# Moving the output weights' block sums beside the second sequence, and its output product to Strassen's form, in a fused attention and SwiGLU kernel

## The chip, the cores and the metric

The kernel runs on one core of one Trainium2 chip. The metric is the time of one execution on the device in microseconds, lower is better. Executions of one kernel agree within about 0.3%. The profile is of one execution: TensorE is PE (PEld its weight loads), VectorE is DVE, ScalarE is ACT, GpSimd is POOL, SyncE, which issues the transfers, is SP.

## The reference, cut to what matters

```python
batch, n_heads, seq, head_dim = (8, 12, 448, 64)
q_n, k_n = rmsnorm(q, g_q), rmsnorm(k, g_k)
scores = scale * q_n @ k_n.T                    # softmax, then @ v
x = attn_out ...reshape(8 * 448, 768)
xn = x / rms(x) * rms_g
g, val = xn @ w_gate, xn @ w_val                # 768 -> 1536
out = (silu(g) * val) @ w_out                   # 1536 -> 768
```

All is in float32. The weights arrive as float64 and are converted on the chip.

## The kernel before

The eight sequences go through a pipeline: while TensorE does the attention of a later sequence, pieces of the feed-forward part of an earlier one are put between ("items"). The first sequence's products are plain, because its weights are still being converted. From the second on, gate and value products are in Strassen's (Winograd's) form, which needs seven block products instead of eight and pays for it with sums and differences of blocks; there are six groups of seven, called quads here. Each quad needs four derived weight blocks (T1 to T4), made on VectorE beside the second sequence, stored to DRAM, and loaded again for every later sequence.

The output product was plain for the first two sequences and in Strassen's form from the third (`FIRST_O = 2`). Its derived blocks, 24 in all, were made in place beside the third sequence:

```python
    FIRST_O = 2
    uses = []                                   # the order in which blocks are loaded
    for b in range(1, B):
        for fp in range(NFP):                   # NFP = 6
            if b == 2:
                uses += [("wd", b, name, fp) for name in BLOCKS]
            uses += [("w", b, fp, name, w) for name in (...) for w in range(2)]
        if b < FIRST_O:
            uses += [("wo", b, *block_of(n, fc)) ...]          # plain: 24 blocks
        else:
            uses += [("wo", b, name, c) for name, _ in out_order(b) for c in range(NFP)]
...
    def derive_o(wait=6):
        ...
        a, b = data(("wd", 2, plus, c)), data(("wd", 2, minus, c))
        nc.vector.tensor_tensor(data(key), a, b, ALU.subtract)
        after(1, store)
```

Strassen's form also needs sums of the hidden blocks, made three items after each quad ends:

```python
        def sums():
            for pair in range(1 + b % 2) if b >= FIRST_O else ():
                ...
                nc.vector.tensor_tensor(of("S1"), of("A21"), of("A22"), ALU.add)
                nc.vector.tensor_tensor(of("S2"), of("S1"), of("A11"), ALU.subtract)
                nc.vector.tensor_tensor(of("S3"), of("A11"), of("A21"), ALU.subtract)
                nc.vector.tensor_tensor(of("S4"), of("A12"), of("S2"), ALU.subtract)
```

In a quad, three PSUM banks go round. VectorE adds each product to running sums (`u` and `cc`, `c` in the profile), which frees its bank; the last product is added by TensorE onto a bank that VectorE must have read before. And the loop that issues an item:

```python
            while asked["derived"] < sums_made:
                derive(0)
                ask()
            pe(fn)
            convert()
            derive()
            derive()
            derive_o()
```

## Time and profile before

| | |
|---|---|
| time, median of the first three runs | 1637.91 us (1637.1 to 1639.52) |
| span of the profile | 1636.9 us |
| TensorE busy | 1615.2 us |
| VectorE, ScalarE, GpSimd busy | 862.6, 499.8, 631.3 us |
| moved by DMA | 273.28 MB |

"Busy" of TensorE is the time covered by its instructions, which overlap. How fast it works is read from how far apart instructions start. The lines are in the prediction.

### The profile page before, as it was taken

What the parts mean: (1) busy time and instruction counts of PE and PEld (TensorE: products, weight loads), DVE (VectorE), ACT (ScalarE), POOL (GpSimd) and SP (SyncE); (2) the same over time, 40 slices, a digit from 0 to 9 for tenths busy, and PEclk for the clock granted to TensorE, in tenths of its full rate; (3) what the DMA queues carried; (4) which work ended last, traced back from release to release, by engine and by line L of the source; (5) the groups of instructions that cost most, each with busy time, mean ns of one, the idle gap of its engine ahead of it and who ended that gap; (6) DMA issues with size and microseconds to landing.
All of it is one profiled execution on the core that took longest, in us unless ns stands there. A gap on an engine that the chain in (4) does not pass through costs nothing.

```text
span 1636.9 us, 21470 instructions
## 1 busy us (share of the span) xinstructions
PE 1615.2 (99%) x7376; PEld 1142.1 (70%) x7376; DVE 862.6 (53%) x1371; ACT 499.8 (31%) x975; POOL 631.3 (39%) x569
## 2 busy tenths in 40 slices
PE   6999999999999999999999999999999999999998
PEld 3444445678855888568875688758876587969984
DVE  6988998366542476426562354624555234433431
ACT  6756563233222332223223222322232123100110
POOL 6777777334423343334433333344343322100000
PEclk9999999999999999999999999999999999999999
DMA  7757674454613866665544655466454464557652
GB/s 195 227 158 204 183 228 128 141 185 142 211 51 117 254 203 222 204 196 162 154 139 120 196 154 159 119 204 192 146 148 124 151 192 114 146 179 241 174 150 65
DMA packets 246443, 273.28 MB, mean 167 GB/s; under 512 B 66356, under 2 KB 243252, under 8 KB 246324
## 3 DMA queue, kind: packets, MB, share of 16 engines
q1 hardware_dynamic: 246004, 271.80, 55.8%
q8 instruction: 61, 1.00, 0.3%
q14 instruction: 58, 0.48, 0.1%
q10 hardware_dynamic: 320, 0.00, 0.0%
HBM read 232.40 MB, written 39.32 MB: 166 GB/s over the span
## 4 chain that ended last, share of the span: by engine, by line
PE 92%; DVE 4%; DMA 2%; ACT 1%; SPq 0%; POOL 0%; issue 0%; DVEq 0%; ACTq 0%; POOLq 0%
PE ff L793 41%; PE ff L987 18%; PE sc L476 9%; PE av L501 8%; PE ff L888 7%; PE den L512 3%; PE ff L1018 2%; PE tr L461 2%; DVE top L646 1%; DVE top L644 1%; DVE top L645 1%; DVE rd L520 1%; DMA qk<-in_k_dram 1%; ACT e L480 1%; DMA raw<-in_moe_w_out_dram 0%; DMA raw<-in_moe_w_gate_dram 0%
## 5 line engine op out<-in xcount | busy, mean ns | idle before, releaser
L793 PE MATMUL ff<-x,w 128*128 128x224 f32 x2016 | 405.7, 353 | 0.0
L793 PEld LDWEIGHTS ff<-x,w 128*128 128x128 f32 x2016 | 378.5, 190 | 12.0 <-issue 6.6
L793 PE MATMUL ff<-xs,w 128*128 128x224 f32 x1512 | 308.0, 353 | 0.0
L793 PEld LDWEIGHTS ff<-xs,w 128*128 128x128 f32 x1512 | 283.4, 190 | 5.3 <-issue 5.3
L480 ACT ACTIVATE e<-sc,rs 112x448 f32<-112x448 f32 x384 | 212.0, 635 | 194.4 <-PE sc L476 189.3
L486 POOL TENSOR_TENSOR es<-e 112x448 f32<-112x448 f32 x82 | 95.1, 1181 | 455.9 <-ACT e L480 455.9
L490 POOL TENSOR_TENSOR es<-es,e 112x448 f32<-112x448 f32 x164 | 187.2, 1152 | 85.3 <-ACT e L480 78.8
L520 DVE RECIPROCAL rd<-rd 128x448 f32<-128x448 f32 x41 | 121.1, 2952 | 143.2 <-ACT rd L519 143.2
L987 PE MATMUL ff<-w,h 128*128 128x384 f32 x576 | 191.1, 487 | 0.0
L476 PE MATMUL sc<-qkT 64*112 64x448 f32 x768 | 179.0, 571 | 5.1 <-ACT qkT L464 5.1
L987 PEld LDWEIGHTS ff<-w,h 128*128 128x128 f32 x576 | 108.1, 190 | 75.5 <-issue 4.0
L501 PE MATMUL av<-e,vt 112*64 112x448 f32 x768 | 154.9, 545 | 0.0
L444 POOL TENSOR_TENSOR rs<-ms,mhalf 112x16 f32<-112x16 f32 (+1 forms) x50 | 143.4, 2867 | 4.2
L476 PEld LDWEIGHTS sc<-qkT 64*112 64x112 f32 x768 | 69.4, 174 | 98.0 <-issue 70.6
L501 PEld LDWEIGHTS av<-e,vt 112*64 112x64 f32 x768 | 50.8, 136 | 95.3 <-issue 75.2
L1018 PE MATMUL ff<-x,w 128*128 128x448 f32 x288 | 112.0, 542 | 0.0
L888 PE MATMUL ff<-w,h 128*128 128x384 f32 x336 | 111.0, 488 | 0.0
L987 PE MATMUL ff<-w,so 128*128 128x384 f32 x324 | 108.6, 488 | 2.0 <-DVE y L948 2.0
L805 DVE TENSOR_TENSOR cc<-ff,u 128x448 f32<-128x448 f32 x84 | 52.4, 624 | 90.4 <-PE ff L793 90.0
L888 PEld LDWEIGHTS ff<-w,h 128*128 128x128 f32 x336 | 62.8, 190 | 43.7 <-issue 2.7
L987 PEld LDWEIGHTS ff<-w,so 128*128 128x128 f32 x324 | 60.5, 190 | 44.7 <-DVE y L948 3.9
L1018 PEld LDWEIGHTS ff<-x,w 128*128 128x128 f32 x288 | 53.3, 190 | 50.8 <-issue 48.8
(86 smaller groups left out, 1470.5 us busy)
## 6 DMA issues: line engine op xcount, KB each, us to landing
w<-kept SPq DMA_DIRECT2D x552, 192.0 KB, 3.3
w<-kept_o SPq DMA_DIRECT2D x318, 192.0 KB, 3.0
kept<-w SPq DMA_DIRECT2D x96, 192.0 KB, 3.8
qk<-in_q_dram SPq DMA_DIRECT2D x48, 224.0 KB, 3.4
qk<-in_k_dram SPq DMA_DIRECT2D x96, 112.0 KB, 3.9
vt<-in_v_dram SPq DMA_DIRECT2D x48, 224.0 KB, 2.8
raw<-in_moe_w_gate_dram SPq DMA_DIRECT2D x24, 384.0 KB, 4.4
raw<-in_moe_w_val_dram SPq DMA_DIRECT2D x24, 384.0 KB, 4.7
```

The lines of the kernel that those rows point to most:

```text
L444: nc.gpsimd.tensor_tensor(st["rs", g][:, cols], ms, mhalf[0:P, cols], ALU.pow)
L476: nc.tensor.matmul(ps[0:P, 0:S], lhsT=qkT[r, 1, c * P:(c + 1) * P], rhs=qkT[r, 0, :], start=True, stop=True)
L480: nc.scalar.activation(e, ps[0:P, 0:S], ACT.Exp, scale=rs[:, n:n + 1])
L486: nc.gpsimd.tensor_tensor(es, st["e", g, 0, j], st["e", g, 1, j], ALU.add)
L490: nc.gpsimd.tensor_tensor(es, es, st["e", g, c, j], ALU.add)
L501: nc.tensor.matmul(av[j * D:(j + 1) * D, 0:S], lhsT=vt[:, j, c, :], rhs=st["e", g, c, j], start=(c == 0), stop=(c == NT - 1))
L520: nc.vector.reciprocal(rd, rd)
L793: nc.tensor.matmul(bank[:, w * HT:(w + 1) * HT], lhsT=wt[:, c * 128:(c + 1) * 128], rhs=x[:, c, :], start=onto is None and w == c == 0, st ...
L805: nc.vector.tensor_tensor(add[name], ps[:, 0:S], add[other], ALU.add)
L888: nc.tensor.matmul(ps, lhsT=st["h", b, fc][:, i * 128:(i + 1) * 128], rhs=data(("wo", b, *block_of(n, fc))), start=(fc == 0), stop=(fc == ...
L987: nc.tensor.matmul(ps, lhsT=a, rhs=data(("wo", b, name, c)), start=first and c == 0, stop=c == NFP - 1, skip_group_check=True)
L1018: nc.tensor.matmul(bank[w][:, 0:S], lhsT=data(key)[:, c * 128:(c + 1) * 128], rhs=st["x", 0, half][:, c, :], start=half == c == 0, stop=ha ...
```

## The change

The intent is to have the output weights' derived blocks one sequence earlier, so that the second sequence's output product takes 84 instead of 96 matmuls. The extra blocks need room, so the four buffers of the weight conversion become block places when the conversion has ended.

```diff
@@ convert
+        if turn_of["n"] == TURNS:
+            free_w.extend(cv_pool.tile([128, BW], F32, name="top") for _ in range(4))
@@
-    FIRST_O = 2
+    FIRST_O = 1
@@ order of loads
-            if b == 2:
+            uses += [("w", b, fp, name, w) for name in (...) for w in range(2)]
+            if b == 1:
                 uses += [("wd", b, name, fp) for name in BLOCKS]
-            uses += [("w", b, fp, name, w) for name in (...) for w in range(2)]
@@ ask
-            if key[1] == 1 and key[0] == "w":
-                keep_free = 7 + 8 * key[2] - asked["derived"]
+            if key[1] == 1 and key[0] in ("w", "wd"):
+                fp = key[2] if key[0] == "w" else key[3]
+                keep_free = max(7 + 8 * fp - asked["derived"], 1)
@@ derive_o: every ("wd", 2, ...) becomes ("wd", 1, ...)
@@ fill
             while asked["derived"] < sums_made:
+                n = asked["derived"]
                 derive(0)
                 ask()
+                if n == asked["derived"]:
+                    pe(idle)
```

More of the change, by code (lines that the diff above doesn't have):

```diff
@@ L706, in safe_scores @@
         for fp in range(NFP):
-            if b == 2:
+            uses += [("w", b, fp, name, w) for name in (("B12", "B11", "B22", "B21") if b == 1 else ORDER) for w in range(2)]
+            if b == 1:
                 uses += [("wd", b, name, fp) for name in BLOCKS]
-            uses += [("w", b, fp, name, w) for name in (("B12", "B11", "B22", "B21") if b == 1 else ORDER) for w in range(2)]
         if b < FIRST_O:
@@ L763, in derive_o @@
         for name in BLOCKS:
-            if asked.get(("wd", 2, name, c), now["t"]) > now["t"] - wait:
+            if asked.get(("wd", 1, name, c), now["t"]) > now["t"] - wait:
                 return
         sums_o.pop(0)
-        a, b = data(("wd", 2, plus, c)), data(("wd", 2, minus, c))
-        key = ("wd", 2, to, c)
-        st[key] = st[("wd", 2, place, c)]
+        a, b = data(("wd", 1, plus, c)), data(("wd", 1, minus, c))
+        key = ("wd", 1, to, c)
+        st[key] = st[("wd", 1, place, c)]
         nc.vector.tensor_tensor(data(key), a, b, ALU.subtract)
@@ L778, in derive_o @@
             for name in ("T1", "T2", "T3", "T4"):
-                after(6, lambda name=name: used(("wd", 2, name, c)))
+                after(6, lambda name=name: used(("wd", 1, name, c)))
     def used(key):
```

## The prediction

> **What bounds the kernel now.** I read the page's first two parts, then the table of what each engine waited for, then the chain that ended last, and then one stage at a time.
>
> ```profile
> span 1636.9 us, 21470 instructions
> ...
> PE 1615.2 (99%) x7376; PEld 1142.1 (70%) x7376; DVE 862.6 (53%) x1371; ACT 499.8 (31%) x975; POOL 631.3 (39%) x569
> ...
> PE tr L461 <- POOL ms L441: 5.5, 1, 5.5
> PE sc L476 <- ACT qkT L464: 5.1, 2, 4.4
> PE ff L987 <- DVE y L948: 2.0, 3, 0.7
> PE tr L461 <- POOL qn L448: 1.9, 1, 1.9
> PE den L512 <- ACT e L480: 1.0, 3, 0.5
> ```
>
> TensorE is idle for 1636.9 - 1615.2 = 21.7 us in all. The waits listed make 15.5 us; the two large ones and the 1.9 us are the very first transposes and scores. The rest, some 6 us, follows the last matmul. Over the 1600 us between, TensorE waits about 3 us. So the time is the sum of what TensorE does, and a change pays by the matmuls it takes out, less any wait that it brings in. No line of this table has TensorE waiting for a weight block's transfer.
>
> What a matmul costs is read from the groups and from the chain, whose columns are start, length, piece:
>
> ```profile
> L793 PE MATMUL ff<-x,w 128*128 128x224 f32 x2016 | 405.7, 353 | 0.0
> L793 PE MATMUL ff<-xs,w 128*128 128x224 f32 x1512 | 308.0, 353 | 0.0
> L987 PE MATMUL ff<-w,h 128*128 128x384 f32 x576 | 191.1, 487 | 0.0
> ...
> L888 PE MATMUL ff<-w,h 128*128 128x384 f32 x336 | 111.0, 488 | 0.0
> ...
> 451.12 7.76 PE ff L888 x24
> ...
> 659.86 7.76 PE ff L987 x24
> ```
>
> The mean of one instruction, 488 ns, is not its cost: neighbours overlap. The cost is the pace, 7.76/24 = 0.323 us for one of 384 columns, the same in the plain product (L888) and in Strassen's form (L987). The trace has each matmul of the program as two instructions: the plain products of sequences 0 and 1 are (3 + 4) x 2 x 12 = 168 matmuls, and the row says 336.
>
> The third reading is by stage: the second sequence's gate and value products (321 to 451 us), its output (to 537), the third sequence's gate and value products (537 to 657), its output, and the fourth's (722 to 842). The columns are stretch, length, busy us of each engine, clock, DMA share and GB/s.
>
> ```profile
> 321.00:451.00 130.00, 130.00 (x697) 110.06 (x696) 79.60 (x125) 38.71 (x77) 54.34 (x51) 1.00 0.58 179
> 451.00:537.00 86.00, 86.00 (x319) 45.76 (x318) 28.89 (x33) 20.30 (x38) 26.15 (x22) 1.00 0.33 95
> 537.00:657.00 120.00, 120.00 (x643) 104.97 (x644) 72.68 (x122) 34.32 (x68) 46.27 (x38) 1.00 0.73 227
> ...
> 722.00:842.00 120.00, 120.00 (x640) 100.05 (x638) 66.15 (x117) 37.85 (x74) 47.57 (x50) 1.00 0.55 158
> ```
>
> TensorE is full in each. VectorE is at 61% where the change will put more on it, and there it is already close behind TensorE at times:
>
> ```profile
> 403.62 0.62 DVE L527 TENSOR_TENSOR x<-av,rd 128x448 f32<-128x448 f32 x1
> 404.17 0.61 DVE L805 TENSOR_TENSOR cc<-ff,u 128x448 f32<-128x448 f32 x1
> 404.70 2.19 DVE L750 TENSOR_TENSOR w<-w,w 128x384 f32<-128x384 f32 x2
> 406.81 0.61 DVE L805 TENSOR_TENSOR c<-ff,u 128x448 f32<-128x448 f32 x1
> ```
>
> There is no idle time before any of these four: for some microseconds VectorE runs behind.
>
> **What the Trainium skill says.** "Perfetto Trace Analysis", section "Tensor Engine Instruction (MATMUL, LD_WEIGHTS)", says that VectorE's queue is strictly first in, first out, and that TensorE's ends are modelled. The first means that an added subtraction delays whatever stands behind it, also a sum that TensorE needs; the four lines above, back to back, agree. "SBUF — State Buffer", section "Who interferes with whom", says that a VectorE instruction with two SBUF inputs contends with a GpSimd instruction that reads SBUF, and one with a single SBUF input does not. All the VectorE work added in the loaded stage has two SBUF inputs. The trace agrees: a pair of block subtractions (L750) takes 2.19 us at 404.70 and 1.02 us at 421.37, and in the fourth sequence a 128x128 sum takes 1.22 us at 766.47 but 0.28 us at 751.41. "DMA: Bandwidth & Descriptors", section "Anatomy of one DMA — SWDGE (gpsimd) path", fits a transfer as 2.0 us plus its bytes at 436 GB/s, which for a 192 KB block would be an estimated 2.45 us; the fit is for the other queue, and the trace's own medians, 3.0 to 3.8 us from issue to landing, are used here.
>
> **The change, part by part.**
> Removed: the plain output product of the second sequence, 4 row tiles x 2 halves x 12 = 96 matmuls. Put in: 2 pairs x 7 products x 6 = 84. The built programs agree: 618 matmuls of 384 columns become 606, and every other matmul count is equal. 12 matmuls x 2 x 0.323 = 7.76 us less TensorE work, all of it on the path; the stage of 86 us should come down to about 78.
> Moved: the 24 subtractions of output weight blocks, their 24 loads and 24 stores go from the third sequence to the second. In the order of the changed program 4 come before the quads of the second sequence and 20 beside them. At the third sequence's rate (20 took 12.8 us of VectorE) that is 12.8 us.
> Added on VectorE: 48 sums of hidden blocks (128x128) for the two pairs, some 40 of them beside those quads. In the fourth sequence 40 such took 3.6 + 4.8 + 4.8 + 3.8 = 17.0 us. VectorE in the second sequence's stage thus goes from 79.6 to about 79.6 + 12.8 + 17.0 = 109 of 130 us, 84%.
> Added transfers: 42 blocks instead of 24 are read for that output, 18 x 0.197 MB = 3.5 MB more over the run. In the stage it is 40 more transfers of 0.197 MB: 7.9 MB on top of 179 GB/s x 130 us = 23.3 MB, about 240 GB/s.
> Four conversion buffers become block places, 27 to 31. By the program's order loads then stand some 40 us of TensorE work ahead of use in the third sequence's quads, before about 23. TensorE waited for none of them, so this buys no time by itself; it makes room for the output blocks among the gate and value blocks. The extra idle steps in the scheduling loop issue no TensorE instruction.
>
> Where can the fuller VectorE hold TensorE? At the product that is added onto a bank after VectorE has read it (B22 onto T1's bank): one product, 6 x 0.379 = 2.3 us, lies between the end of T1 and that need, and the addition takes 0.6 us, so a lag of 1.7 us is free. In the order of the changed program the tightest place is the fifth quad. There VectorE has, from u2 up to that addition: u2 0.53, eight sums 3.4, an output block 0.64, u3 0.53, two halves of the hidden block 0.7, two derived blocks 1.3, a transpose's copy 0.53, the addition 0.53, together 8.2 us. TensorE gets from u2's place to the need in 8.0 us, and about 1.3 us of earlier work is still queued then. So a wait of about 1.5 us is due there; by the same count about half of that in the third quad, and around zero in the others. A GpSimd collision can double any of these instructions. I put the new waits at 2 us, estimated from these rows, with 0.5 to 5 as reasonable.
>
> Sum: 1637.9 - 7.8 + 2.0 = 1632.1 us.
>
> **Rivals.**
> VectorE becomes the bound of the second sequence. For: 84% of a strict queue, with two thirds of the derived blocks in bursts, and every GpSimd collision lengthens it. Against: in the stretch from 82 to 123 us VectorE is busy for 36.5 of 41 us and TensorE does not idle. If all the margin went, 5 to 8 us of waits would cancel the gain: 1635 to 1638.
> The transfers become the bound. For: about 240 GB/s in a stage where VectorE itself waits for blocks, so a late block stops its whole queue. Against: 227 GB/s over the third sequence's 120 us stood beside a full TensorE, and in the changed order the shortest distance from a load to its subtraction is 7 to 8 us there, while landing took 3.7 to 5.3 us. The exceptions, 2 to 3 us for the first subtractions, come some 25 us before TensorE needs them; VectorE waited 4.8 us at that place before as well, harmlessly. If it happened: 1633 to 1637.
> The gain is all kept, 1630.1: if the burst of sums falls into free time, as it does in the fourth sequence, where L793 has no idle at all.
>
> **Range and chances.** Runs of the kernel before spread from 1637.1 to 1639.5. The lower end is the full gain with a favourable run, 1629; the upper end, 1635.5, has the gain eaten by five microseconds of waits. 2% is 33 us, over four times what was taken out, and nothing in the profile can lose as much: 1% faster, 97% within, 2% slower.
>
> **What would show it.** Right: 1,068 Strassen output instructions and 144 plain ones; the second sequence's output stage about 78 us; VectorE near 109 us between 321 and 451; new TensorE waits of 0.5 to 5 us in all, put down to the VectorE addition (cc) and lying between 340 and 435 us; everything after shifted earlier by 5 to 8 us with the stage lengths unchanged. Wrong: TensorE waiting for weight blocks, a second sequence over 135 us, or a pace of the added products that isn't 0.323 us.

## The result, and the profile after

| | before | changed |
|---|---|---|
| median, six runs each on the same chip | 1638.61 us | 1631.05 us |
| lowest to highest | 1637.07 to 1639.56 | 1630.26 to 1632.68 |
| span of the profile | 1636.9 | 1629.0 |
| TensorE busy | 1615.2 | 1607.8 |
| VectorE busy | 862.6 | 871.8 |
| moved by DMA | 273.28 MB | 276.83 MB |

The ratio is 0.9957, 95% interval 0.9944 to 0.997. A ratio is the mean time of one kernel's runs over that of the other's in the same rounds, so it is not quite the ratio of the medians. 0.43% is faster beyond the noise, and "the same" at 2%.

The span and busy times of the changed kernel's page, and, from its table of waits, everything that TensorE waited for (us in total, times, longest):

```profile
span 1629.0 us, 21534 instructions
...
PE 1607.8 (99%) x7352; PEld 1136.8 (70%) x7352; DVE 871.8 (54%) x1425; ACT 499.9 (31%) x975; POOL 632.7 (39%) x569
```

```profile
PE tr L461 <- DMA qk<-in_k_dram: 4.9, 1, 4.9
PE sc L476 <- ACT qkT L464: 3.9, 2, 3.2
PE tr L461 <- POOL qn L448: 2.6, 1, 2.6
PE ff L991 <- DVE y L952: 2.0, 3, 0.7
PE ff L797 <- DVE u L809: 0.8, 1, 0.8
PE ff L797 <- DVE cc L809: 0.4, 1, 0.4
PE den L512 <- ACT e L480: 0.4, 1, 0.4
```

TensorE has 24 instructions fewer. Apart from the first transposes and scores, where the waits change from run to run, there are two new waits against before, both of a quad's product (L797) for a VectorE addition, 0.8 and 0.4 us. No line names a transfer of a weight block. The groups of the output products, plain (L892) and Strassen (L991), count the replacement:

```profile
L991 PE MATMUL ff<-w,h 128*128 128x384 f32 x594 | 202.8, 487 | 0.0
...
L991 PE MATMUL ff<-w,so 128*128 128x384 f32 x338 | 117.3, 488 | 1.4 <-DVE y L952 1.4
...
L892 PE MATMUL ff<-w,h 128*128 128x384 f32 x144 | 47.7, 488 | 0.0
...
L991 PE MATMUL ff<-top,h 128*128 128x384 f32 x78 | 31.9, 490 | 0.0
...
L991 PE MATMUL ff<-top,so 128*128 128x384 f32 x58 | 23.6, 488 | 0.7 <-DVE y L952 0.7
```

594 + 338 + 78 + 58 = 1068 Strassen instructions and 144 plain ones. The name "top" is that of the four new places.

The times of stages are best read from the starts of instructions, because ends are modelled. I use three marks in the timeline of TensorE: the first quad matmul of the second sequence, its first output matmul, and the first output matmul of the third sequence. Stage A is the second sequence's quads; stage B its output product and the third sequence's quads together. B is taken as one because the attention pieces slid across the border between them: the output part alone went from 85.9 to 70.8 us, the quads after it from 122.8 to 130.2.

| | first mark | stage A | stage B |
|---|---|---|---|
| before | 320.72 | 130.24 us | 208.74 us |
| changed | 318.74 | 132.02 us | 201.01 us |

The lines of the three marks, first before and then in the changed kernel:

```profile
320.72 2.45 PE L793 MATMUL ff<-x,w 128*128 128x224 f32 x12
...
450.96 7.92 PE L888 MATMUL ff<-w,h 128*128 128x384 f32 x24
...
659.70 7.92 PE L987 MATMUL ff<-w,h 128*128 128x384 f32 x24
```

```profile
318.74 1.31 PE L797 MATMUL ff<-x,w 128*128 128x224 f32 x6
...
450.76 0.82 PE L991 MATMUL ff<-w,h 128*128 128x384 f32 x2
...
651.77 7.92 PE L991 MATMUL ff<-w,h 128*128 128x384 f32 x24
```

Stage B is 7.73 us shorter, which is the saved matmuls; stage A is 1.78 us longer. Together that is 5.95 us. The other 2 us between the two profiles lie ahead of the first mark, where TensorE has the same work in both: over the profiles, that mark falls anywhere between 317.5 and 321.7 us. So the change is worth about 6 us by the stages. The medians of this pair show 7.6, most likely because they carry the chance of the start as well; the interval of the ratio (4.9 to 9.2 us) holds both.

Where stage A loses its time is in the third quad. First VectorE's timeline in the changed kernel (start, length, instruction, and in brackets the idle time before it), then two lines of GpSimd's, then TensorE's:

```profile
365.31 2.95 DVE L520 RECIPROCAL rd<-rd 128x448 f32<-128x448 f32 x1 [0.40 <-ACT rd L519]
368.36 0.62 DVE L527 TENSOR_TENSOR x<-av,rd 128x448 f32<-128x448 f32 x1
368.90 1.05 DVE L872 TENSOR_TENSOR so<-h,h 128x128 f32<-128x128 f32 x1
370.06 1.49 DVE L873 TENSOR_TENSOR so<-so,h 128x128 f32<-128x128 f32 x1
371.46 1.22 DVE L874 TENSOR_TENSOR h<-h 128x128 f32<-128x128 f32 x1
372.61 0.28 DVE L875 TENSOR_TENSOR so<-h,so 128x128 f32<-128x128 f32 x1
...
373.74 0.55 DVE L754 TENSOR_TENSOR w<-top,w 128x384 f32<-128x384 f32 x1
...
375.14 0.62 DVE L809 TENSOR_TENSOR u<-ff,p 128x448 f32<-128x448 f32 x1
...
378.49 0.61 DVE L809 TENSOR_TENSOR u<-ff,u 128x448 f32<-128x448 f32 x1
...
381.39 0.61 DVE L809 TENSOR_TENSOR cc<-ff,u 128x448 f32<-128x448 f32 x1
```

```profile
366.36 4.64 POOL L490 TENSOR_TENSOR es<-es,e 112x448 f32<-112x448 f32 x4 [1.94 <-ACT e L480]
...
371.32 1.22 POOL L533 TENSOR_TENSOR ss<-ss,rd 128x448 f32<-128x448 f32 x1
```

```profile
379.15 2.54 PE L797 MATMUL ff<-x,w 128*128 128x224 f32 x12 [0.81 <-DVE u L809]
382.06 2.54 PE L797 MATMUL ff<-xs,w 128*128 128x224 f32 x12 [0.37 <-DVE cc L809]
384.43 0.55 PE L461 MATMUL tr<-ident,qk 112*128 112x112 f32 x4
```

VectorE has no idle time from the reciprocal at 365.31 to the addition that ends at 382.0. The first sums of hidden blocks take 1.05, 1.49 and 1.22 us instead of 0.28: GpSimd's four additions of the softmax sums run from 366.36 to 371.0 and another from 371.32 to 372.5. Behind the eight sums and up to the second `u` stand nine subtractions, three of output weight blocks (L774) and six for the quads (L754). Each addition that TensorE needs comes out late. The first wait is for the bank that the second `u` frees; the second is for the `cc` that must be read before the last product.

The idle times shown, 0.81 and 0.37, make 1.18 us; the stage lost 1.78. The dozen behind the second wait is drawn as 2.54 us, but the next instruction starts 2.37 us after it did; a dozen with no break before it is drawn as 2.43 us (at 387.11) and followed after 2.27. So a drawn end lies some 0.17 us late, each wait is shown that much too short, and the dozen behind a break takes 0.10 us longer. A wait thus costs some 0.27 us more than is shown, which makes 1.7 of the 1.78 us.

### The profile page after: what moved, and what is told of

The parts are those of the page before. It is cut to its first block, busy times and chain, and to the rows that moved or that the text cites. A ratio compares the mean times of both kernels' runs of the same rounds, so it can differ in the third digit from the quotient of the medians.

```text
span 1629.0 us, 21534 instructions
## 1 busy us (share of the span) xinstructions
PE 1607.8 (99%) x7352; PEld 1136.8 (70%) x7352; DVE 871.8 (54%) x1425; ACT 499.9 (31%) x975; POOL 632.7 (39%) x569
## 2 busy tenths in 40 slices
DMA packets 249036, 276.83 MB, mean 170 GB/s; under 512 B 66644, under 2 KB 245844, under 8 KB 248916
## 4 chain that ended last, share of the span: by engine, by line
PE 91%; DVE 5%; DMA 2%; ACT 1%; SPq 0%; issue 0%; POOL 0%; DVEq 0%; ACTq 0%; POOLq 0%
PE ff L797 40%; PE ff L991 21%; PE sc L476 9%; PE av L501 9%; PE den L512 3%; PE ff L892 3%; PE ff L1022 2%; PE tr L461 2%; DVE top L646 1%; DVE top L644 1%; DVE rd L520 1%; DVE top L645 1%; ACT e L480 1%; DMA qk<-in_k_dram 1%; DMA raw<-in_moe_w_out_dram 0%; DMA raw<-in_moe_w_gate_dram 0%
## 5 line engine op out<-in xcount | busy, mean ns | idle before, releaser
L797 PE MATMUL ff<-x,w 128*128 128x224 f32 x1728 | 352.3, 354 | 0.8 <-DVE u L809 0.8
L797 PEld LDWEIGHTS ff<-x,w 128*128 128x128 f32 x1728 | 324.1, 190 | 12.1 <-issue 8.6
L797 PE MATMUL ff<-xs,w 128*128 128x224 f32 x1326 | 272.5, 353 | 0.4 <-DVE cc L809 0.4
L797 PEld LDWEIGHTS ff<-xs,w 128*128 128x128 f32 x1326 | 248.7, 190 | 5.4 <-issue 4.7
L991 PE MATMUL ff<-w,h 128*128 128x384 f32 x594 | 202.8, 487 | 0.0
L520 DVE RECIPROCAL rd<-rd 128x448 f32<-128x448 f32 x41 | 121.0, 2952 | 137.6 <-ACT rd L519 137.6
L991 PEld LDWEIGHTS ff<-w,h 128*128 128x128 f32 x594 | 111.5, 190 | 76.6 <-issue 2.7
L991 PE MATMUL ff<-w,so 128*128 128x384 f32 x338 | 117.3, 488 | 1.4 <-DVE y L952 1.4
L991 PEld LDWEIGHTS ff<-w,so 128*128 128x128 f32 x338 | 63.2, 190 | 45.9 <-DVE y L952 2.6
L427 DVE TENSOR_REDUCE ms<-sq 112x8 f32<-112x512 f32 x96 | 61.2, 677 | 52.6 <-ACT sq L424 52.6
L1022 PEld LDWEIGHTS ff<-x,w 128*128 128x128 f32 x288 | 53.3, 190 | 50.9 <-issue 49.0
L682 POOL TENSOR_TENSOR w<-top,raw 128x384 int32<-128x384 int32 x72 | 78.5, 1105 | 25.1 <-DVE top L646 7.3
```

Source lines behind the costliest of these rows:

```text
L427: nc.vector.tensor_reduce(out=ms[:, i * n:(i + 1) * n], in_=sq.rearrange("p (n d) -> p n d", d=D), axis=AX_X, op=ALU.add)
L520: nc.vector.reciprocal(rd, rd)
L682: nc.gpsimd.tensor_tensor(data(key).bitcast(I32), top, lo, ALU.add)
L797: nc.tensor.matmul(bank[:, w * HT:(w + 1) * HT], lhsT=wt[:, c * 128:(c + 1) * 128], rhs=x[:, c, :], start=onto is None and w == c == 0, st ...
L991: nc.tensor.matmul(ps, lhsT=a, rhs=data(("wo", b, name, c)), start=first and c == 0, stop=c == NFP - 1, skip_group_check=True)
L1022: nc.tensor.matmul(bank[w][:, 0:S], lhsT=data(key)[:, c * 128:(c + 1) * 128], rhs=st["x", 0, half][:, c, :], start=half == c == 0, stop=ha ...
```

## The experiments

Theory A is the prediction's: the gain is TensorE's 24 fewer instructions, and the cost is VectorE's fuller queue beside the second sequence. Rivals: blocks arriving earlier give part of the gain (B); the moved subtractions are what costs (C); the new places are not needed (D); the waits are a chance (E); work taken from VectorE comes back through GpSimd (F). Ten runs were made, each kernel in five rounds (e3_no_places has a sixth run) beside the kernel before. "Waits" are the listed ones of the quads' products for VectorE, "VectorE in A" its busy time between the marks of stage A; all in us. Both stages come from the profile of one execution each.

| run | stage A | stage B | VectorE in A | waits | median | ratio to before |
|---|---|---|---|---|---|---|
| before | 130.24 | 208.74 | 79.6 | 0 | | |
| changed | 132.02 | 201.01 | 100.7 | 1.2 | 1631.05 | 0.9957 |
| e0_changed_again | 132.02 | 201.00 | 100.8 | 1.2 | 1631.73 | 0.9962 |
| e1_places_only | 130.24 | 208.75 | 80.9 | 0 | 1638.20 | 1.0004 |
| e2_move_only | 130.24 | 208.74 | 90.8 | 0 | 1637.83 | 0.9999 |
| e3_no_places | 145.16 | 201.00 | 104.1 | 11.1 | 1644.77 | 1.0043 |
| e4_more_vector | 145.76 | 201.00 | 121.0 | 11.3 | 1648.04 | 1.0064 |
| e5_sums_spread | 132.04 | 201.00 | 100.8 | 1.3 | 1632.18 | 0.9960 |
| e6_subs_gpsimd | 134.47 | 201.00 | 103.3 | 2.3 | 1634.58 | 0.9975 |
| e7_sums_gpsimd | 131.42 | 201.01 | 94.0 | 0.7 | 1631.82 | 0.9956 |
| e8_subs_yield | 130.24 | 201.00 | 101.7 | 0 | 1630.73 | 0.9953 |
| e9_yield_gpsimd | 130.24 | 201.00 | 92.7 | 0 | 1629.89 | 0.9950 |

All intervals of the ratios are about 0.0013 wide to either side. All results were correct. Medians are compared only through the ratio; the stage lengths repeat to 0.02 us wherever the instructions are the same.

**The changed kernel again**, for the second call's comparisons.

> The changed kernel itself, as the measure for the other three of this call: 1631 within 1 us, ratio to before 0.9955.

It came as expected, with the same two waits and the same stages. The two waits are thus no chance of one run.

**The places alone.** The kernel before, with the lines of the change that extend `free_w`.

```diff
+        if turn_of["n"] == TURNS:
+            free_w.extend(cv_pool.tile([128, BW], F32, name="top") for _ in range(4))
```

> The kernel before, with the four conversion buffers given to the weight blocks and nothing else. Theory A (the gain is TensorE's 24 fewer instructions, 7.8 us, less what the fuller VectorE makes it wait in the second sequence, some 1.2 to 1.8 us): no gain, ratio to before 1.000 within 0.0007, and no TensorE wait for a weight block, as before. Rival B (a good part of the gain is that blocks arrive earlier): 2 us or more faster than before.

Nothing gained, both stages to 0.01 us as before: rival B falls.

**The move alone.** The changed kernel with the second sequence's output left plain.

```diff
-    FIRST_O = 1
+    FIRST_O = 2
```

> The changed kernel with the second sequence's output product left plain: the weight subtractions are moved to the second sequence and the places are there, but no matmul is saved and no sums of hidden blocks are made for it. Theory A: time as before, 1638.6 within 1 us; VectorE about 93 us busy in the 130 us of the second sequence's gate and value products (79.6 before, 100 in the changed kernel); TensorE waits there 0.3 us at most. Rival B: 2 us or more faster than before. Rival C (the move of the subtractions and their transfers is what costs 1.8 us in the changed kernel, not the sums): 1.5 us or more slower than before, with the wait near 380 us still there.

Both stages are those of before. The 20 subtractions and their transfers cost nothing although they lengthen VectorE's work in the stage to 91 us and raise the DMA rate there from 179 to 243 GB/s. Rival C falls: the 1.78 us come only when the sums of hidden blocks join them. In the third quad the same nine subtractions stand ahead of the second `u` here, without the eight sums, and TensorE does not wait for it. That also shows that the transfers do not hold TensorE at this rate.

**No places.** The changed kernel without the extension of `free_w`.

```diff
-            free_w.extend(cv_pool.tile([128, BW], F32, name="top") for _ in range(4))
```

> The changed kernel without the four conversion buffers as places. In its order of instructions two pairs of subtractions for the second sequence's quads stand directly before the quad that needs them (third and fifth quad), so there TensorE has to wait for VectorE. Theory A: TensorE's work is as in the changed kernel (1631), plus 1.5 to 4 us at each of the two places, so 1634 to 1638; the waits are for subtractions of weight blocks. Rival D (the places are not needed): 1631 within 1 us.

The direction was right and the size was not: 1644.77 us, slower than the kernel before. Its longest wait from the table of waits, then the stretch of six microseconds in which the first of the two ends (stretch, length, busy us by engine, granted clock, DMA share, GB/s), then TensorE's timeline there:

```profile
PE ff L794 <- DVE w L751: 11.1, 2, 5.5
```

```profile
374.00:380.00 6.00, 3.71 (x11) 3.40 (x12) 5.01 (x13) 0.00 (x0) 0.49 (x1) 0.52 0.36 130
```

```profile
368.23 2.54 PE L794 MATMUL ff<-x,w 128*128 128x224 f32 x12
376.29 4.23 PE L794 MATMUL ff<-xs,w 128*128 128x224 f32 x12 [5.53 <-DVE w L751]
380.36 4.70 PE L794 MATMUL ff<-x,w 128*128 128x224 f32 x24
```

TensorE waited 5.5 us twice for a subtraction (L751) that stood in VectorE's queue behind a reciprocal and the eight sums. When it went on, the granted clock was low, 0.52 on the mean of these six microseconds: the twelve instructions after the wait took from 376.29 to 380.36, 4.07 us instead of 2.27. Two waits of 5.53 us and two slow dozens, which lost 1.8 and 1.7 us, are 14.6 of the 14.92 us that the stage lost; twice the 0.17 us by which a wait is shown short makes the rest. So the places do no good by themselves, but without them the derived blocks are made so late that the change loses about 7 us (ratio 1.0043) instead of gaining. Rival D falls.

**More work on VectorE.** Three needless subtractions ahead of each output weight subtraction.

```diff
+        junk = tmp.tile([128, 128], F32, name="junk", tag="junk", bufs=1)
+        for i in range(3):
+            nc.vector.tensor_tensor(junk, a[:, i*128:(i+1)*128], b[:, i*128:(i+1)*128], ALU.subtract)
         nc.vector.tensor_tensor(data(key), a, b, ALU.subtract)
```

> The changed kernel with three needless 128x128 subtractions on VectorE ahead of each of the 24 output weight subtractions: about 60 x 0.25 = 15 us more on VectorE in the second sequence's 130 us, which makes about 115 of 130. Theory A: VectorE's queue is what makes TensorE wait, so the waits grow from 1.2 us to 4 to 10 us, at additions (u, cc) of the quads, and the time to 1634 to 1640. Rival E (the 1.2 us were a chance collision with GpSimd and VectorE still has room): within 1 us of the changed kernel.

The waits grew ten times, at the additions that were expected, and cost more than expected: 1648.04 us.

```profile
PE ff L800 <- DVE u L812: 8.9, 5, 2.8
...
PE ff L800 <- DVE cc L812: 2.4, 4, 1.8
```

Some 18 us more of VectorE's work lengthened the stage by 13.7 us against the changed kernel, by 15.5 us against before. Of the 15.5 us, 11.3 are listed; nine times the 0.27 us that a listed wait leaves out make 2.4 us more. Of the remaining 1.8 us, 1.5 are a lower clock behind the longest wait, 2.76 us: the two dozens that start at 388.07 and 391.95 us are drawn as 3.60 and 2.94 us, where the dozens behind the other waits are drawn as 2.54. Rival E falls: in this order of the queue VectorE has no more room in this stage. Whether it has in another order is a different question, which e8_subs_yield answers.

**Sums in two halves.** The second pair's sums three items later, to break the burst of eight.

```diff
+                if pair and b == 1:
+                    after(3, add_up)
+                else:
+                    add_up()
```

> The changed kernel with the second pair's four sums in the second sequence made three TensorE steps after the first pair's, so that no eight stand together. Theory A (VectorE's lag against TensorE is what costs): the wait in the third quad shrinks or goes if the burst makes it, and the time falls by up to 1.5 us below the changed kernel's. If the lag is made by the reciprocal and the weight subtractions around it rather than by the burst, the waits stay at 0.5 to 2 us and the time is the same within 0.7 us; by counting the work in the order I expect this second outcome.

The same stage to 0.02 us, as I expected of this one. The three sums that collide with GpSimd belong to the first half, and the second half lands behind the first `u` but still ahead of the second, at 376.49 to 377.4, so nothing is taken out of the stretch before the addition that TensorE waits for.

**Output weight subtractions on GpSimd.**

```diff
-        nc.vector.tensor_tensor(data(key), a, b, ALU.subtract)
+        nc.gpsimd.tensor_tensor(data(key), a, b, ALU.subtract)
```

> The changed kernel with the 24 output weight subtractions on GpSimd. Theory A: VectorE falls from 100 to about 89 us in the second sequence's 130 us, the waits of TensorE there fall to 0.5 us or less, and the time to 1629.5 to 1630.5. Rival F (GpSimd's reads hold up VectorE's two-input additions, so that what leaves one queue comes back as longer instructions): the mean of VectorE's two-input subtractions rises by a third or more and the time stays at 1631 or above.

Rival F is right, though the rise is 32% and not the full third that was named. VectorE has 20 subtractions, 11 us, less in the stage and is busy for 103 us nevertheless: the mean of the commonest subtractions for quads (L754 w<-w,w) rises from 609 to 805 ns, and in the third quad six of the eight sums take over 1 us instead of three. And the wait in that quad, 2.28 us, is again followed by a slow clock:

```profile
376.00:380.00 4.00, 1.72 (x11) 1.43 (x10) 4.00 (x6) 0.63 (x1) 2.24 (x2) 0.96 0.23 88
380.00:384.00 4.00, 4.00 (x15) 3.71 (x14) 3.96 (x9) 0.00 (x0) 0.25 (x2) 0.61 0.95 288
384.00:388.00 4.00, 4.00 (x23) 3.95 (x22) 1.77 (x4) 0.39 (x1) 3.92 (x3) 1.00 1.03 358
```

The busy column of TensorE says 4.00 of 4.00 in the middle line, and its count and clock say that it worked at little over half its pace.

**Sums on GpSimd.**

```diff
+                eng = nc.gpsimd if b == 1 else nc.vector
-                nc.vector.tensor_tensor(of("S1"), ...)      # and the other three
+                eng.tensor_tensor(of("S1"), ...)
```

> The changed kernel with the second sequence's 48 sums of hidden blocks on GpSimd. Theory A: VectorE falls from 100 to about 83 us in the second sequence's 130 us, near the 79.6 of before, TensorE waits there 0.3 us at most, and the time is 1629 to 1630.5. Rival F: VectorE's two-input subtractions get longer by a third or more, or GpSimd's queue delays the norm of the next pair, and the time stays at 1631 or above.

In between: VectorE falls to 94 us, not 83, because its subtractions get longer: the commonest for output weights go from 552 to 768 ns, the commonest for quads from 609 to 754. GpSimd's get longer too: its four additions in the third quad take 5.37 us, and 4.64 in the changed kernel. The waits fall to 0.7 us, the stage gains 0.6 us, and the time is the changed kernel's within the noise.

**The two kinds of subtraction kept apart.** The work is the same; an output weight subtraction goes into the queue only after an item that brought no subtraction for the quads.

```diff
+            n = asked["derived"]
             derive()
             derive()
-            derive_o()
+            if n == asked["derived"]:
+                derive_o()
```

> The changed kernel, but an output weight subtraction is put into VectorE's queue only after a TensorE item that brought no subtraction for the quads, so that the two kinds don't stand in one burst; the work of every engine is the same. Theory A, in its sharper form (what costs is VectorE's lag in the gapless stretch of the third quad, not its total work): the second sequence's gate and value stage is again 130.2 to 130.8 us long instead of 132.0, and the time 0.5 to 1.8 us below the changed kernel's, about 1630; VectorE's busy time stays near 100 us. If the total work is what costs, the stage stays at 131.5 us or more.

The stage is 130.24 us again, exactly that of before, with VectorE as busy as in the changed kernel:

```profile
319.00:451.00 132.00, 132.00 (x705) 111.44 (x705) 101.95 (x184) 39.35 (x77) 57.11 (x54) 1.00 0.69 218
```

TensorE is busy for 132.00 of 132.00. In the third quad the sums collide with GpSimd as before. But between the last of them and the second `u` there stand three subtractions, where the changed kernel has nine:

```profile
375.29 0.28 DVE L875 TENSOR_TENSOR so<-h,so 128x128 f32<-128x128 f32 x1
375.49 0.55 DVE L774 TENSOR_TENSOR w<-w,w 128x384 f32<-128x384 f32 x1
375.95 0.62 DVE L809 TENSOR_TENSOR u<-ff,p 128x448 f32<-128x448 f32 x1
376.49 0.55 DVE L774 TENSOR_TENSOR w<-w,w 128x384 f32<-128x384 f32 x1
377.07 0.56 DVE L774 TENSOR_TENSOR w<-top,w 128x384 f32<-128x384 f32 x1
377.55 0.62 DVE L809 TENSOR_TENSOR u<-ff,u 128x448 f32<-128x448 f32 x1
```

The three are the output weights' (L774); the six that left are those for the quads (L754). So the edit did not thin the stretch in the way that it was written for: it held the output weights' subtractions back, and the quads' moved behind the `cc`, presumably since blocks now come free at other times. Six times 0.47 us, the pace at which they follow each other, is 2.8 us less ahead of that addition. What cost 1.78 us is thus the place of about 3 us of work in the queue, not the sum of the work. Together with e2_move_only, which has the nine subtractions and no sums, both sides are tested: with the sums away or with the six subtractions away TensorE does not wait. No run takes away GpSimd's collision and nothing else, so its share is not shown.

**Both.** The last edit and the sums on GpSimd.

> The same, with the second sequence's sums of hidden blocks on GpSimd besides. If the lag is gone already with the first edit, this brings nothing more: stage within 0.4 us of that one's, time within 0.7 us. If GpSimd's reads are what lengthens VectorE's queue, it is worse, 131 us or more.

The stages are the same to 0.01 us; nothing is added, as expected.

Both versions are 7.7 us shorter in the two stages than the kernel before and 1.8 us shorter than the changed one. Their ratios to before, 0.9953 and 0.9950, beat the kernel before for sure; against the changed kernel (0.9957, 0.9962) the intervals overlap, so that advantage is shown by the stage lengths alone, not by the total time.

## Why the prediction was right

The predicted time was 1632.1 us, a change of -5.8 us; the stages show -5.95, the ratio -7.0 with 2.1 to either side.

The bound: TensorE's work sets the time, and every profile here agrees; stage B is 201.00 to 201.01 us in all nine runs with that output product in Strassen's form and 208.74 or 208.75 without.

Removed: 24 instructions at a pace of 0.323 us were to give 7.76 us; 7.73 came. That the output stage would be about 78 us and the later stages unchanged in length was not so by the marks: the output part shrank by 15.1 us and the next quads grew by 7.4, since the attention pieces are dealt out by share of work. Only the sum was right, and only the sum matters.

Moved and added on VectorE: 109 us of 130 were predicted, 100.3 measured between the same two times (321 to 451 us). The forty sums took 5.3 + 4.7 + 4.3 + 2.8 = 17.1 us by their groups, as predicted. The twenty subtractions were over-sized: 11.0 us instead of 12.8, and the quads' own forty came down from 25.9 to 24.6 us. Most of the rest is overlap, which busy time counts once while the groups count it in each: in this window the groups add up to 84.0 us before and to 110.2 after, against 79.6 and 100.3 us of busy time, so the overlap grew from 4.4 to 9.9 us.

New waits: 2 us were predicted, 1.78 came, in the quads and behind VectorE's additions as said. But the place was wrong: the fifth quad was to give 1.5 us and the third half of that, while the third gave all and the fifth none. The step that failed is "eight sums 3.4" us, one average for all quads. In the fifth quad they take 1.9 us, for no GpSimd addition runs beside them:

```profile
415.97 0.27 DVE L872 TENSOR_TENSOR so<-h,h 128x128 f32<-128x128 f32 x1
...
417.69 0.28 DVE L875 TENSOR_TENSOR so<-h,so 128x128 f32<-128x128 f32 x1
417.89 0.55 DVE L774 TENSOR_TENSOR w<-w,w 128x384 f32<-128x384 f32 x1
418.36 0.62 DVE L809 TENSOR_TENSOR u<-ff,u 128x448 f32<-128x448 f32 x1
```

From the start of the first sum to that of the subtraction behind the eighth that is 415.97 to 417.89. The whole stretch from that quad's first `u` to the end of the `cc` addition took 6.2 us and not the 8.2 that were counted. In the third quad the same eight take from 368.90 to 373.74, 4.8 us, since they come right behind an attention block, when GpSimd adds up the softmax sums. The prediction had named the collision as a risk for any instruction, but not looked where it must fall, which the order shows: behind the reciprocal. The total came out right because what was too much in one quad made up for what was too little in the other; that is luck, since a wait doesn't grow evenly with the work ahead of it.

The first wait was also of a kind that the prediction did not name: the bank that `u` frees, not the bank that is added onto.

The rivals: that VectorE would become the bound was closest to happening; some 18 us more on its queue cost 13.7 us of time. The transfers did not hold TensorE at 233 GB/s. The gain all kept is what the two last versions show.

"It buys no time by itself" was right of the places (no gain alone), but the prediction did not see what they are for: without them the change loses about 7 us.

## What to carry to other kernels

When an engine off the critical path gets more work, its share of busy time does not tell what it costs: at 100.7 and at 101.7 us of the same stage it cost 1.78 us or nothing, depending on which 3 us of work stood ahead of an addition that TensorE needed. Look in the order for the stretch without a gap, count what stands in it between two results that the bound engine needs, and let work that nobody is waiting for yield there. Handing such work to an engine that contends with the first can make both longer.

## What the Trainium skill lacked or had wrong

- "TensorE: Matmul & The Clock Gate", section "HAM oscillation — how this bites in real kernels", gives as the rule no TensorE gaps over some 3.4 us. Here a listed wait of 2.28 us was followed by a granted clock of 0.61 over four microseconds, while one of 2.26 us in another run was followed by 1.00 (stretches of four microseconds). In the six microseconds in which each of the two waits of 5.5 us ended the clock was 0.52 and 0.55 on the mean, and twelve instructions took 4.07 us instead of 2.27, somewhat less than the 4.5 us that the page's half clock would make of them.
- "Perfetto Trace Analysis", section "Tensor Engine Instruction (MATMUL, LD_WEIGHTS)", says that TensorE's ends are modelled, but not by how much: here twelve matmuls were drawn as 2.54 us behind a break and the next started after 2.37, or as 2.43 without one and the next started after 2.27, so each idle time reads about 0.17 us short.
- "SBUF — State Buffer", section "Who interferes with whom", says who contends, but it gives its two slowdowns (VectorE 6.8 times, GpSimd 1.5 times) without the instructions that they were measured on. Here a 128x128 sum took 0.28 us alone and 1.05 to 1.49 us beside GpSimd's additions of 1.16 us each, and moving 11 us of subtractions to GpSimd lengthened VectorE's commonest other ones from 609 to 805 ns. The page's section "SBUF: two separate sides" says that whichever starts first holds the shared ports for its whole instruction. In the fifth quad GpSimd's power of 112x16 values, which has two SBUF inputs, is drawn from 414.51 for 3.28 us, and VectorE's sums beside it from 415.97 on took 0.28 us each (in the kernel before likewise: a power from 749.60 for 2.91 us, a sum of 0.28 us at 751.41); GpSimd's drawn spans are rough, so this is an observation, not a proof.
